# One decode step of attention and a gated feed-forward layer on one core: output weights in eight pieces, feed-forward weights behind all values, down projection in rows

## Chip, cores, metric

The kernel runs on one core of one Trainium2 chip. The metric is device time in microseconds (us) of one execution; most quoted times are medians of 4 to 9 runs. A ratio is the mean time of one kernel's runs over that of the other's runs of the same rounds, so it is not quite the ratio of the medians quoted. Each comes with a 95% interval, and the intervals here are about ±0.13% (±1.7 us) wide.

## The reference

Batch 4, one query token, 32 heads of width 128, 8192 cached keys and values per head, all in bf16. The formulas are shortened from the reference.

```python
def _A_ref(x, k_cache, v_cache, wq, wo):            # D = 512, H = 32, Dh = 128, Sk = 8192
    q = (x @ wq).reshape(B, 1, H, Dh).transpose(0, 2, 1, 3)
    scores = jnp.einsum("bhqd,bhkd->bhqk", q, k_cache) * (Dh ** -0.5)
    o = jnp.einsum("bhqk,bhkd->bhqd", _softmax(scores), v_cache)
    return o.transpose(0, 2, 1, 3).reshape(B, 1, H * Dh) @ wo

def _B_ref(x, w_gate, w_up, w_down):                # F = 1792
    return (_sigmoid(x @ w_gate) * (x @ w_up)) @ w_down

h  = x + _A_ref(_layernorm(x), k_cache, v_cache, wq, wo)
h2 = h + _B_ref(_layernorm(h), w_gate, w_up, w_down)
```

The caches are 537 MB and everything else is 14 MB: 128 key tiles and 128 value tiles of 2 MB each (one per batch and head), 4 MB each of query and output weights, 1.8 MB each of gate, up and down weights.

## The kernel before

All big loads are issued by one queue (the sync engine, SP), in the order of the list `items`. Keys, values and most weights go through a ring of eight 2 MB slots; the load of an item waits until the earlier tenants of its slot have been used up. A value is loaded ten steps (`LAG`) behind the key of the same head. The output weights are put where the transposed keys were (`kT`), so their load waits for the last score.

```python
        items = [("wq", 0)]
        for t in range(NT + LAG):                   # NT = 128, LAG = 10
            if t < NT:
                items.append(("k", t))
            if t == NT + 3:
                items.append(("wo", 0))             # after value 120
            if t == NT + LAG - 1:
                items.append(("wg", 0))             # ahead of the last value
            if t >= LAG:
                items.append(("v", t - LAG))
        items += [("wu", 0), ("wd", 0)]
        # ... ring slots ...
            if kind == "wo":
                return [(lambda e: e.dma_start(wo_v, A_wo.rearrange("(h p) f -> p h f", p=128)).then_inc(s_wo, 16),
                         s_wo, 16)]
            # ... the last value (127) comes in four pieces, all else in one load each ...
        for it in items:
            for op in dma_of[it]:
                op.deps = [sc_of[NT - 1]] if it[0] == "wo" else [consumed[p] for p in prev_of[it]]
```

The end of the program works on transposed activations: a feature on a partition, the batch of 4 in the columns. So in the down projection the weights are the stationary operand and only 4 columns move; the sum is added to `h`, turned round by four transposes, and cast.

```python
        def pe_down(e):
            mm = None
            for c in range(NDC):                    # 4
                for t in range(NFT):                # 14
                    mm = e.matmul(bX[:, B * c:B * c + B], wd_v[:, t, 128 * c:128 * (c + 1)],
                                  hh_sb[:, B * t:B * t + B], start=(t == 0), stop=(t == NFT - 1))
            return mm
        p_d = P("pe", pe_down, [d_hh, dma_of[("wd", 0)][0], d_st])
        d_o = P("dve", lambda e: e.tensor_tensor(oT_f[:, :], h2[:, 0, :], bX[:, 0:NB], ALU.add), [p_d])
        # ... pe_oT: four transposes of oT_f into bP[0] ...
        d_out = P("dve", lambda e: e.tensor_copy(o_sb[:, :], bP[0][0:B, 0:D]), [p_oT])
```

Of the kernel before, what the change touches and what calls it, by code (L numbers as in the profile page):

```python
# [6 lines left out]
FP32 = mybir.dt.float32  # L7
U32 = mybir.dt.uint32
ALU = mybir.AluOpType
ACT = mybir.ActivationFunctionType  # L10
AX = mybir.AxisListType

GH = 8
LAG = 10
# [58 lines left out]
def bass_sequential_preLN__mha_block_cached__glu_gated_glu__decode_kernel(  # L73
# [12 lines left out]
    B, _sq, D = A_x.shape  # L86
    _, H, S, DH = A_k_cache.shape
# [3 lines left out]
    NDC = D // 128  # L91
    NFT = F // 128
    NT = B * H
    NG = NT // GH
    R = S // 128
    TW = R * 128
# [4 lines left out]
    P = prog.add  # L101

    with ExitStack() as es:
        def SB(name, shape, dt):
            return es.enter_context(nc.sbuf_tensor(name, shape, dt))
# [9 lines left out]
        identf = SB("identf", [128, 128], FP32)  # L115
# [6 lines left out]
        x_bf = SB("x_bf", [128, D], BF16)  # L122
# [13 lines left out]
        h2 = SB("h2", [128, 2, NDC * B], FP32)  # L136
# [2 lines left out]
        hnT = SB("hnT", [128, NDC * B], BF16)  # L139
        sg_sb = SB("sg_sb", [128, NFT * B], FP32)  # L140
        hh_sb = SB("hh_sb", [128, NFT * B], BF16)
        oT_f = SB("oT_f", [128, NDC * B], FP32)
        o_sb = SB("o_sb", [B, D], BF16)

        PS = es.enter_context(nc.psum_tensor("PS", [128, 4096], FP32))
# [1 line left out]
        bS, bO, bP = bank[0:2], bank[2:4], bank[4:6]  # L147
        bX, bH = bank[6], bank[7]

        sems = {e: SEM("s_" + e) for e in _Prog.ENGS}  # L150
        s_x = SEM("s_x")
        s_out = SEM("s_out")
        s_wo = SEM("s_wo")
        s_slot = [SEM(f"s_slot{i}") for i in range(NS)]
        s_piece = [SEM(f"s_piece{i}") for i in range(4)]

        def ringv(slot):
            return ring[:, slot, :]


        items = [("wq", 0)]
        for t in range(NT + LAG):
            if t < NT:
                items.append(("k", t))
            if t == NT + 3:
                items.append(("wo", 0))
            if t == NT + LAG - 1:
                items.append(("wg", 0))
            if t >= LAG:
                items.append(("v", t - LAG))  # L170
        items += [("wu", 0), ("wd", 0)]
        slot_of, prev_of, dma_of = {}, {}, {}
        owner = [None] * (NS - 1) + [("qr", 0)]
        uses = [0] * NS
# [12 lines left out]
        consumed = {}  # L187
# [3 lines left out]
        wo_v = kT[:, :, :].rearrange("p s f -> p (s f)").rearrange("p (h f) -> p h f", h=H)  # L191
        wg_v = ringv(slot_of[("wg", 0)])[:, 0:NDC * F].rearrange("p (c f) -> p c f", c=NDC)
        wu_v = ringv(slot_of[("wu", 0)])[:, 0:NDC * F].rearrange("p (c f) -> p c f", c=NDC)
        wd_v = ringv(slot_of[("wd", 0)])[:, 0:NFT * D].rearrange("p (t f) -> p t f", t=NFT)

        def kv_src(t, cache):
            return cache[t // H, t % H, :, :].rearrange("(p r) d -> p (r d)", p=128)

        dma_x = P("sp", lambda e: e.dma_start(x_bf[0:B, :], A_x.rearrange("b s d -> (b s) d")).then_inc(s_x, 16),
                  sem=s_x, val=16)  # L200

        def load(it):
            kind, t = it
            slot = slot_of.get(it)
            if kind == "wo":
                return [(lambda e: e.dma_start(wo_v, A_wo.rearrange("(h p) f -> p h f", p=128)).then_inc(s_wo, 16),
                         s_wo, 16)]
            if kind == "v" and t == NT - 1:
                ops = []
                for i in range(4):  # L210
                    def f(e, i=i):
                        c0 = i * (TW // 4)
                        return e.dma_start(ringv(slot)[:, c0:c0 + TW // 4],  # L213
                                           kv_src(t, A_v_cache)[:, c0:c0 + TW // 4]).then_inc(s_piece[i], 16)
                    ops.append((f, s_piece[i], 16))
                return ops
            uses[slot] += 1
            sem, val = s_slot[slot], 16 * uses[slot]
            if kind == "k":
                dst, src = ringv(slot), kv_src(t, A_k_cache)  # L220
            elif kind == "v":
                dst, src = ringv(slot), kv_src(t, A_v_cache)
            elif kind == "wq":
                dst, src = wq_v, A_wq.rearrange("(c p) f -> p c f", p=128)
            elif kind == "wg":
                dst, src = wg_v, B_w_gate.rearrange("(c p) f -> p c f", p=128)
            elif kind == "wu":
                dst, src = wu_v, B_w_up.rearrange("(c p) f -> p c f", p=128)
            else:
                dst, src = wd_v, B_w_down.rearrange("(t p) f -> p t f", p=128)  # L230
            return [(lambda e: e.dma_start(dst, src).then_inc(sem, 16), sem, val)]  # L231


# [72 lines left out]
        for half in range(2):  # L306
            for a in range(4):
                def f(e, half=half, a=a):
                    dst = bass.AP(ring, QR0 + half * 2048 + 32 * a,
                                  [[NS * TW, 128], [256, 8], [128, 2], [1, 32]])  # L310
                    src = bS[half][:, :].rearrange("p (g w e) -> p g e w", g=8, e=2)
                    if half == 0:
                        return e.activation(dst, src, ACT.Copy)
                    return e.tensor_copy(dst, src)  # L314
# [15 lines left out]
        for b in range(B):  # L330
            ops = []
# [54 lines left out]
        def pe_pv(t, r0=0, r1=R, last=True):  # L386
            it = ("v", t)
            g, hh = t // GH, t % GH
            slot = slot_of[it]
            ob = bO[(g + (1 if t == NT - 1 else 0)) % 2]  # L390

            def f(e):
                mm = None
                for r in range(r0, r1):
                    c0 = (r % 16) * 32 + (r // 16) * 8 + hh
                    mm = e.matmul(ob[:, hh:hh + 1], ringv(slot)[:, r * 128:(r + 1) * 128],  # L396
                                  PT_sb[:, g % 2, c0:c0 + 1], start=(r == 0), stop=(r == R - 1))
                return mm
            deps = [ptc_of[g]]
            if t == NT - 1:  # L400
                deps += [dma_of[it][r0 // 16]]
            else:
                deps += dma_of[it]
            if hh == 0:
                deps.append(oev_of.get(g - 2))
            if t == NT - 1:
                deps.append(oev_of.get(g - 1))
            op = P("pe", f, deps)
            if last:
                pv_of[t] = op  # L410
                consumed[it] = op
# [105 lines left out]
        def wo_mms(e, heads, b0, b1, first=False):  # L517
            mm = None
            for h in heads:
                for c in range(NDC):  # L520
                    mm = e.matmul(bH[:, c * B + b0:c * B + b1], wo_v[:, h, 128 * c:128 * (c + 1)],
                                  OT[:, b0 * H + h:(b1 - 1) * H + h + 1:H],
                                  start=(first and h == heads[0] and c == 0),
                                  stop=(h == H - 1 and c == NDC - 1), skip_group_check=True)
            return mm
        gl = NG - 1
        P("pe", lambda e: wo_mms(e, range(0, H - GH), 0, B, True), [oev_of[gl - 1], dma_of[("wo", 0)][0], d_xnT])
        if B > 1:
            P("pe", lambda e: wo_mms(e, range(H - GH, H), 0, B - 1), [oev_of[gl - 1]])
        o_a = oev(gl, 0, GH - 1)  # L530
        P("pe", lambda e: wo_mms(e, range(H - GH, H - 1), B - 1, B), [o_a])
        P("act", lambda e: e.activation(lnst[0:B, 9:10], lnst[0:B, 3:4], ACT.Sqrt), [exp_of[gl]])
        for i in range(4):
            pe_pv(NT - 1, 16 * i, 16 * i + 16, last=(i == 3))
        o_b = oev(gl, GH - 1, GH)
        p_attn = P("pe", lambda e: wo_mms(e, range(H - 1, H), B - 1, B), [o_b])

# [21 lines left out]
                                                  mean_b(20), ALU.mult), [d_rs, d_hc])  # L559
        P("act", lambda e: e.activation(lnst[0:B, 10:11], tst[0:B, 12:13], ACT.Sigmoid), [a_sq])  # L560

        def pe_gu(e, wv, bk):
            mm = None
            for t in range(NFT):
                for c in range(NDC):
                    mm = e.matmul(bk[:, B * t:B * t + B], wv[:, c, 128 * t:128 * (t + 1)],
                                  hnT[:, B * c:B * c + B], start=(c == 0), stop=(c == NDC - 1))
            return mm
# [2 lines left out]
        a_sig = P("act", lambda e: e.activation(sg_sb[:, :], bS[0][:, 0:NFT * B], ACT.Sigmoid), [p_g])  # L571
        d_hh = P("dve", lambda e: e.tensor_tensor(hh_sb[:, :], sg_sb[:, :], bS[1][:, 0:NFT * B], ALU.mult), [a_sig, p_u])

        def pe_down(e):
            mm = None
            for c in range(NDC):
                for t in range(NFT):
                    mm = e.matmul(bX[:, B * c:B * c + B], wd_v[:, t, 128 * c:128 * (c + 1)],  # L578
                                  hh_sb[:, B * t:B * t + B], start=(t == 0), stop=(t == NFT - 1))
            return mm  # L580
        p_d = P("pe", pe_down, [d_hh, dma_of[("wd", 0)][0], d_st])
        d_o = P("dve", lambda e: e.tensor_tensor(oT_f[:, :], h2[:, 0, :], bX[:, 0:NB], ALU.add), [p_d])

        def pe_oT(e):
            mm = None
            for c in range(NDC):
                mm = e.transpose(bP[0][0:B, 128 * c:128 * (c + 1)], oT_f[:, B * c:B * c + B], identf[:, :])  # L587
            return mm
        p_oT = P("pe", pe_oT, [d_o, ptc_of[gl], ptc_of[gl - 1]])
        d_out = P("dve", lambda e: e.tensor_copy(o_sb[:, :], bP[0][0:B, 0:D]), [p_oT])  # L590
        consumed[("wg", 0)] = consumed[("wu", 0)] = consumed[("wd", 0)] = p_d

        def sp_out(e):
            e.dma_start(out.rearrange("b s d -> (b s) d"), o_sb[:, :]).then_inc(s_out, 16)
            return e.wait_ge(s_out, 16)
        P("sp", sp_out, [d_out])

        for it in items:
            for op in dma_of[it]:
# [51 lines left out]
```

## Time and profile before

The first lines are from the page of the kernel before: the span of the profiled execution, the busy time of the engines, the row of the queue that fetches instructions (packets, MB, share of the time of the 16 DMA engines), and the chain of work that ended last, by engine.

```profile
span 1314.9 us, 24889 instructions
PE 522.6 (40%) x11846; PEld 327.6 (25%) x11846; DVE 629.1 (48%) x640; ACT 38.9 (3%) x86; POOL 9.7 (1%) x17
...
q8 instruction: 92, 1.51, 0.5%
...
DMA 82%; DVE 12%; issue 3%; SPq 2%; PE 1%
```

The chain is 82% DMA, and TensorE and VectorE are busy less than half of the time. A kernel that is bound like this, and has to load the same bytes, gets faster in two ways only: the DMA engines must lose less time, or less must be left to do after the last byte.

The next two lines are the DMA view of 1180 to 1316 us in 40 slices of 3.4 us: busy tenths of the DMA engines, and GB/s.

```profile
DMA  9999999999999995699975999999999999998300
GB/s 429 419 424 429 436 429 414 429 429 419 439 424 424 429 424 246 252 393 381 366 251 192 354 437 429 434 419 429 429 429 411 398 396 390 411 388 292 138 0 1
```

There are two holes, at slices 16 and 17 (about 1231 to 1238 us) and at slices 21 and 22 (1248 to 1255 us). The timeline of the same kernel shows the issues that belong to them (start, duration, engine, load):

```profile
1235.66 0.38 SPq L206 DMA_DIRECT2D kT<-in_A_wo_dram  x1
1236.08 20.89 SPq L231 DMA_DIRECT2D ring<-in_A_v_cache_dram  x6
```

The output weights are issued only when the last score is done (1235.66 us), and all loads behind them in the queue wait too. Of the six value loads in the second line, the first alone holds the queue for 18.3 us, until 1254.4 us. By then 3298 of the 4096 rows (1 KB each) of the output weights have started in the trace; that its descriptors wait for theirs to drain is my reading.

The holes invite the thought that some 6 us of loading are lost there (four slices of 3.4 us at a mean of 235 instead of 428 GB/s). The trace holds one more thing that says otherwise. Each load leaves sixteen completion records, one per DMA engine. (The Trainium skill, "DMA: Bandwidth & Descriptors", section "Why a DMA increments its semaphore by 16 and not by 1", says that each of the sixteen engines adds one when its share has landed.) Sorted, they read as follows in the kernel before:

| load | first eight engines land (us) | last eight engines land (us) |
|---|---|---|
| key 0 | 18.0 to 18.1 | 18.2 to 18.6 |
| value 119 | 1226.3 to 1232.4 | 1241.8 to 1244.0 |
| value 120 | 1231.2 to 1237.2 | 1246.7 to 1249.0 |
| output weights | 1249.8 to 1250.1 | 1257.8 to 1260.0 |
| value 121 | 1261.0 to 1261.8 | 1262.8 to 1264.9 |
| value 127, last piece | 1295.1 to 1296.2 | 1298.6 to 1300.2 |
| up weights | 1299.6 to 1300.7 | 1303.3 to 1304.8 |
| down weights | 1304.7 to 1305.7 | 1308.0 to 1309.4 |

Eight engines run ahead of the other eight (the records do not name the engine; that it is the same eight each time is inferred from the order). From the first to the last it is 17.7 us at value 119. Both holes are idle time of the early half. The late half goes from load to load without a gap: while the holes last (1231.5 to 1236.6 and 1249.5 to 1254.4 us) the packets keep the 16 engines 59 and 54% busy, about nine of them. A load counts only when its last engine has landed. I call the two groups the early and the late half.

Last, the chain of waits from 1285 us on (start, duration, what):

```profile
1285.71 23.72 DMA ring<-in_B_w_down_dram
1309.44 0.14 issue
1309.57 1.65 PE PS L578 x56
...
1311.24 0.18 DVE oT_f L582
...
1311.47 1.02 PE PS L587 x4
...
1312.52 0.68 DVE o_sb L590
```

After the down weights have landed (1309.44 us) there are 1.65 us of down projection (56 matmuls), 0.18 of addition, 1.02 of transposes and 0.68 of cast. The output is issued at 1313.23 us, 3.79 us after the landing.

### The profile page before, as it was taken

Reading aid. Unit: us, or ns where it says so; the run is one execution under the profiler, and the core shown is the slowest. Engines: PE = TensorE matmul, PEld = TensorE weight load, DVE = VectorE, ACT = ScalarE, POOL = GpSimd, SP = SyncE. Lnnn points to the kernel's source line nnn. Section 1 sums busy time; section 2 is a strip of 40 time slices with the busy share of each in tenths; the row PEclk is TensorE's granted clock in tenths of the full one; section 3 lists DMA queues with packets and bytes.
Section 4 is the critical chain, followed back from the end, with each engine's and each line's share of the span. In section 5 each row is a group of like instructions: output and inputs, shape, how many; then the busy total and the mean of one; then the engine's idle time right before and its main releaser. Section 6 shows DMA issues by size and latency. Waiting matters only on the chain.

```text
span 1314.9 us, 24889 instructions
## 1 busy us (share of the span) xinstructions
PE 522.6 (40%) x11846; PEld 327.6 (25%) x11846; DVE 629.1 (48%) x640; ACT 38.9 (3%) x86; POOL 9.7 (1%) x17
## 2 busy tenths in 40 slices
PE   2453443433343353343344344344334434334425
PEld 1122222222232232222222222222222223222324
DVE  6975445445444544544544454554544444454300
ACT  3000000000000000000000000000000000000000
POOL 2000000000000000000000000000000000000000
DMA  9999999999999999999999999999999999999997
GB/s 391 428 427 426 428 426 428 426 426 427 427 427 427 428 427 425 427 427 428 426 427 428 427 426 428 426 428 427 426 427 427 426 428 425 429 426 428 371 381 292
DMA packets 44917, 552.37 MB, mean 420 GB/s; under 512 B 4232, under 2 KB 10128, under 8 KB 11664
## 3 DMA queue, kind: packets, MB, share of 16 engines
q1 hardware_dynamic: 44816, 550.79, 99.1%
q8 instruction: 92, 1.51, 0.5%
q14 instruction: 9, 0.07, 0.0%
HBM read 550.77 MB, written 0.00 MB: 419 GB/s over the span
## 4 chain that ended last, share of the span: by engine, by line
DMA 82%; DVE 12%; issue 3%; SPq 2%; PE 1%
DMA ring<-in_A_k_cache_dram 77%; DVE kT L356 11%; DMA ring<-in_A_v_cache_dram 2%; DMA ring<-in_B_w_down_dram 2%; SPq L213 1%; DMA ring<-in_A_wq_dram 1%; DVE Lq L339 0%; SPq L231 0%; PE PS L396 0%; PE PS L373 0%; PE PS L297 0%; DVE ring L314 0%; PE PS L324 0%; PE PS L578 0%; PE PS L587 0%
## 5 line engine op out<-in xcount | busy, mean ns | idle before, releaser
L356 DVE STREAM_TRANSPOSE kT<-ring 128x1024 uint32<-128x1024 uint32 x512 | 592.3, 1213 | 596.0 <-DMA ring<-in_A_k_cache_dram 596.0
L373 PE MATMUL PS<-kT,Lq 128*32 128x512 bf16 x2048 | 242.8, 623 | 663.5 <-DVE kT L356 663.5
L396 PEld LDWEIGHTS PS<-PT_sb,ring 128*128 128x128 bf16 x8192 | 230.1, 104 | 116.1 <-issue 75.5
L396 PE MATMUL PS<-PT_sb,ring 128*128 128x1 bf16 x8192 | 239.3, 165 | 39.7 <-DMA ring<-in_A_v_cache_dram 36.5
L373 PEld LDWEIGHTS PS<-kT,Lq 128*32 128x32 bf16 x2048 | 56.8, 126 | 751.3 <-DVE kT L356 679.8
L435 ACT ACTIVATE negm<-PS 128x1 f32<-128x1 f32 x16 | 2.7, 171 | 1166.9 <-PE PS L431 1166.9
L446 PE MATMUL PS<-LS,onesf 128*128 128x8 f32 x32 | 9.5, 372 | 65.2 <-DVE LS L442 65.2
L468 DVE TENSOR_TENSOR OT<-PS,rinv 128x8 bf16<-128x8 f32 (+2 forms) x17 | 2.0, 115 | 53.4 <-PE PS L396 53.4
L446 PEld LDWEIGHTS PS<-LS,onesf 128*128 128x128 f32 x32 | 8.0, 311 | 66.8 <-DVE LS L442 66.8
L457 PE MATMUL PS<-Sel,E_sb 128*32 128x32 bf16 x1024 | 11.4, 193 | 2.5 <-issue 1.4
L414 DVE TENSOR_REDUCE mx<-PS 128x1 f32<-128x512 f32 x16 | 10.5, 657 | 2.0 <-PE PS L373 2.0
L431 PEld LDWEIGHTS PS<-onesf,rowx 1*128 1x128 f32 x32 | 8.0, 307 | 12.6 <-issue 12.6
L437 ACT ACTIVATE E_sb<-PS,negm 128x512 bf16<-128x512 f32 x16 | 11.0, 687 | 0.7 <-ACT negm L435 0.2
L463 ACT ACTIVATE PT_sb<-PS 128x512 bf16<-128x512 f32 x16 | 9.6, 597 | 27.0 <-PE PS L457 27.0
L457 PEld LDWEIGHTS PS<-Sel,E_sb 128*32 128x32 bf16 x1024 | 9.6, 103 | 2.8 <-issue 1.5
L431 PE MATMUL PS<-onesf,rowx 1*128 1x1 f32 x32 | 9.3, 358 | 0.0
L249 POOL MEMSET Lq<- 128x8208 f32 x1 | 6.9, 6937 | 0.0
L339 DVE CAST Lq<-PS 32x128 bf16<-32x128 f32 x8 | 5.7, 712 | 2.2 <-PE PS L324 2.0
L267 DVE TENSOR_SCALAR xpad<-x_bf,lnst 4x512 bf16<-4x512 bf16 x1 | 6.0, 5993 | 0.0
L420 PE MATMUL PS<-identf,mx 128*1 128x128 f32 x16 | 5.9, 371 | 0.0
L314 DVE CAST ring<-PS 128x512 bf16<-128x512 f32 x4 | 2.5, 684 | 7.2 <-PE PS L297 7.2
L338 ACT ACTIVATE Lq<-PS 32x128 bf16<-32x128 f32 x8 | 5.7, 715 | 4.3 <-PE PS L324 4.1
(69 smaller groups left out, 67.5 us busy)
## 6 DMA issues: line engine op xcount, KB each, us to landing
ring<-in_A_k_cache_dram SPq DMA_DIRECT2D x128, 2048.0 KB, 34.7
ring<-in_A_v_cache_dram SPq DMA_DIRECT2D x127, 2048.0 KB, 35.9
ring<-in_A_wq_dram SPq DMA_DIRECT2D x1, 4096.0 KB, 12.5
kT<-in_A_wo_dram SPq DMA_DIRECT2D x1, 4096.0 KB, 24.3
ring<-in_A_v_cache_dram SPq DMA_DIRECT2D x4, 512.0 KB, 28.0
ring<-in_B_w_gate_dram SPq DMA_DIRECT2D x1, 1792.0 KB, 37.8
ring<-in_B_w_up_dram SPq DMA_DIRECT2D x1, 1792.0 KB, 23.4
ring<-in_B_w_down_dram SPq DMA_DIRECT2D x1, 1792.0 KB, 23.7
```

Of the source, the lines that this page charges most:

```text
L213: return e.dma_start(ringv(slot)[:, c0:c0 + TW // 4], kv_src(t, A_v_cache)[:, c0:c0 + TW // 4]).then_inc(s_piece[i], 16)
L249: zlq = pool(lambda e: e.memset(Lq[:, :].bitcast(FP32), 0.0))
L267: d_x = P("dve", lambda e: e.tensor_scalar(xpad[0:B, :], x_bf[0:B, :], st[0:B, 0:1], st[0:B, 4:5], op0=ALU.subtract, op1=ALU.mult), [d_r, zx])
L356: return e.transpose(kT[:, buf, i * q:(i + 1) * q].bitcast(U32), ringv(src)[:, i * q:(i + 1) * q].bitcast(U32))
L373: mm = e.matmul(bS[g % 2][32 * j:32 * (j + 1), :], Lq[:, l0:l0 + 32], rhs, start=(hh == 0 and v == 0), stop=(hh == GH - 1 and v == 3), til ...
L396: mm = e.matmul(ob[:, hh:hh + 1], ringv(slot)[:, r * 128:(r + 1) * 128], PT_sb[:, g % 2, c0:c0 + 1], start=(r == 0), stop=(r == R - 1))
L414: mx_of[g] = P("dve", lambda e: e.tensor_reduce(mx[:, :], bS[g % 2][:, :], AX.X, ALU.max), [sc_of[g * GH + GH - 1], p1_of.get(g - 1)])
L431: p2_of[g] = P("pe", lambda e: e.matmul(bX[:, 0:1], rowx[0:1, :], onesf[0:1, 0:1], start=True, stop=True), [d2b_of[g], c_ones])
L437: exp_of[g] = P("act", lambda e: e.activation(E_sb[:, :], bS[g % 2][:, :], ACT.Exp, bias=negm[:, 0:1], scale=SCALE, accum_out=sig[:, 0:1]) ...
L446: L_of[g] = P("pe", lambda e: e.matmul(bX[:, 0:GH], onesf[:, :], LS[:, :], start=True, stop=True), [LS_of[g], a1_of[g], c_ones])
L457: mm = e.matmul(bP[g % 2][32 * a:32 * (a + 1), 32 * rr:32 * rr + 32], E_sb[:, 32 * rr:32 * rr + 32], Sel[:, a, :], start=True, stop=True, ...
L463: ptc_of[g] = P("act", lambda e: e.activation(PT_sb[:, g % 2, :], bP[g % 2][:, :], ACT.Copy), [pt_of[g]] + last_pv)
```

## The change

Its intent: fill the holes (output weights in eight pieces between the last values, so that no value is stuck behind 4096 descriptors), let the last value come before the feed-forward weights, and shorten the end (no transposes: the down projection makes rows of the output directly, on top of `h`, which TensorE has put into the same accumulator beforehand; ten of the fourteen tiles of the down weights can be used before the rest has landed). The core of the diff, with cuts:

```diff
+        WD_PARTS = [(0, 10), (10, NFT)]
+        NWO = 8
+        HW = H // NWO
         ...
             if t < NT:
                 items.append(("k", t))
-            if t == NT + 3:
-                items.append(("wo", 0))
-            if t == NT + LAG - 1:
-                items.append(("wg", 0))
             if t >= LAG:
                 items.append(("v", t - LAG))
-        items += [("wu", 0), ("wd", 0)]
+            if NT + 1 <= t <= NT + NWO:
+                items.append(("wo", t - NT - 1))
+        items += [("wg", 0), ("wu", 0), ("wd", 0)]
         ...
-        dma_x = P("sp", lambda e: e.dma_start(x_bf[0:B, :], ...
+        dma_x = P("act", lambda e: e.dma_start(x_bf[0:B, :], ...
         ...   (wo: eight loads of four heads; value 127: two pieces instead of four; wd: two loads)
+        def pe_h(e):
+            mm = None
+            for s_ in range(2):
+                for c in range(2):
+                    k = 2 * s_ + c
+                    mm = e.matmul(bP[s_][0:B, 128 * c:128 * (c + 1)], h2[:, 0, B * k:B * k + B], identf[:, :],
+                                  start=(c == 0), stop=False, skip_group_check=True)
+            return mm
         ...
-        (pe_down in 56 matmuls, d_o, pe_oT, d_out)
+        p_d = []
+        for i, (t0, t1) in enumerate(WD_PARTS):
+            for s_ in range(2):
+                def pe_down(e, t0=t0, t1=t1, s_=s_):
+                    mm = None
+                    for t in range(t0, t1):
+                        mm = e.matmul(bP[s_][0:B, 0:HD], hh_sb[:, B * t:B * t + B], wd_v[:, t, HD * s_:HD * s_ + HD],
+                                      start=False, stop=(t == NFT - 1), skip_group_check=True)
+                    return mm
+                p_d.append(P("pe", pe_down, [d_hh, dma_of[("wd", 0)][i]]))
+        o0 = P("act", lambda e: e.activation(o_sb[:, 0:HD], bP[0][0:B, 0:HD], ACT.Copy), [p_d[2]])
+        o1 = P("dve", lambda e: e.tensor_copy(o_sb[:, HD:D], bP[1][0:B, 0:HD]), [p_d[3]])
```

In the new form the four columns of `hh` are the stationary operand and 256 columns (HD) of the weights move, in 28 matmuls.

## The prediction

> **What bounds the kernel now.** The page of the profile shows 552 MB at a mean of 420 GB/s, DMA share 9 in all slices but the last; the chain of waits is 82% DMA. So only lost DMA time and the work after the last byte can be won. The sixteen completion records of each load split the DMA engines into two halves: early they land together (18.0 to 18.6 us), but value 120 lands on eight engines at 1231-1237 us, on the other eight at 1247-1249. I put the drift down to instruction fetches (92 packets of 16 KB) on one half. The late half has no gap: value 120 at 1249.0, output weights 1260.0, value 121 at 1264.9, ..., last piece of the last value 1300.2, up weights 1304.8, down weights 1309.4. It sets the end.
>
> **The loads.** In the DMA table by slices the rate falls to 190-250 GB/s at about 1230-1237 and 1247-1254 us: the large output-weight load waits for the last score (1235.7), and the next value's issue is stuck 18.3 us behind its descriptors. Eight pieces cure the second hole, but both are idle time of the early half, off the critical path. The first even grows by one value (4.9 us), since the first piece queues behind value 119 instead of 120; the late half still has work until about 1244. Reordering leaves the late half's sum unchanged. Small terms: query weights issue 0.4 us earlier (-0.4); 1 KB descriptors run at 46 instead of 43.5 ns beside a busy other half (estimate, +0.4); six more completions (+0.3). Last byte: 1309.7 instead of 1309.4.
>
> **The tail after it.** Before (timeline): landing 1309.44, 56 matmuls with 4 moving columns to 1311.22 (28 ns each), add 0.17, transposes 1.0, cast 0.68, output issue 1313.23: 3.8 us. The change removes add, transposes and half of the cast, but makes the down projection 28 matmuls that stream 256 columns. The score matmuls stream 512 and start, in groups of four side by side, every 0.427 us in all 128 bursts, so 256 cost about 0.213 us (estimate). The Trainium skill ("TensorE: Matmul & The Clock Gate", Part 1) gives 1.2 GHz for a cold array and 2.4 after some 3.4 us of sustained work; the trace agrees with the cold figure (512 columns in 0.427 us) and shows no faster burst. 28 x 0.213 = 6.0 us against 1.6. The first 20 can start about 1.4 us before the last landing: -1.4 + 0.1 + 6.0 + 0.2 drain + 0.5 cast = 5.4 us until the output's issue when cold, about 2.4 if warm throughout. I take 4.8, as the array may warm within the burst: +1.0. Adding h in PSUM and the later feed-forward weights sit in slack.
>
> **Sum.** +1.0 (tail) +0.3 (last byte) = +1.3: 1318.3 us, range 1315.4 to 1320.4. Chances: faster by over 2% 0.01, within 2% 0.98, slower 0.01.
>
> **What would show it.** Right: the second rate hole is gone, the first longer; the last landing within 1 us of 1309.4; down-projection matmuls spaced 0.21 us or falling to 0.11; output issue 4 to 5.4 us after the landing. Wrong: the last landing moves by several us (the hole had slowed the late half), or matmuls at 0.11 us from the start (about 1316).
>
> **What would make it wrong.** A warm array (-2.5); the late half running dry behind the pieces' waits (several us); an instruction fetch stalling the tail (+2).

## The result and the profile after

The changed kernel took 1317.93 us (median of 4 runs, 1317.60 to 1318.59) against 1317.01 us (median of 4, 1316.99 to 1317.26); ratio 1.0007, interval 0.999 to 1.0024. By the interval that is "the same". All four runs of the change are slower than all four of before, so the sign is probable.

The lines of the page that answer to those above:

```profile
span 1316.8 us, 24848 instructions
PE 527.4 (40%) x11822; PEld 330.1 (25%) x11822; DVE 628.7 (48%) x639; ACT 39.2 (3%) x87; POOL 9.7 (1%) x17
...
q8 instruction: 92, 1.51, 0.5%
...
DMA 85%; DVE 12%; issue 2%; PE 1%; SPq 0%
```

The profiled run was the slowest of the four (1318.59 us), so its span is 1.9 us longer, while the medians differ by 0.9. The DMA slices of 1180 to 1316 us:

```profile
DMA  9999999999999754699999999999999999988400
GB/s 439 419 424 426 429 419 429 434 424 429 429 419 429 337 241 212 246 425 397 425 398 423 404 418 401 409 405 397 427 383 422 389 414 406 387 300 270 143 4 1
```

The second hole is gone and the first has become longer (slices 14 to 17 instead of 16 and 17), as the first piece of the output weights now queues behind value 119 and not behind value 120. The issues:

```profile
1235.67 0.38 SPq L207 DMA_DIRECT2D kT<-in_A_wo_dram  x1
1236.09 0.51 SPq L241 DMA_DIRECT2D ring<-in_A_v_cache_dram  x1
...
1237.11 3.69 SPq L241 DMA_DIRECT2D ring<-in_A_v_cache_dram  x1
```

No value load holds the queue for 18 us any more; the longest of these takes 6.0. Still, the landings of the late half at the end are where they were: up weights at 1305.3 us (before: 1304.8), last part of the down weights at 1310.05 (before: 1309.44). The chain from there:

```profile
1286.08 22.63 DMA ring<-in_B_w_down_dram
1308.70 0.14 issue
1308.84 5.76 PE PS L602 x28
...
1314.62 0.41 DVE o_sb L607
```

The first part of the down weights lands at 1308.70 us, 28 matmuls take 5.76 us, and the output is issued at 1315.13, 5.08 us after the last landing (before: 3.79). What the transposes gave, the long stream took.

The windows view of the down-projection line alone shows how (stretch in us, its length, busy time of TensorE and number of matmuls, the same for weight loads, granted clock, DMA share, GB/s):

```profile
1309.50:1310.50 1.00, 1.00 (x6) 0.57 (x5) 0.50 0.00 1
1310.50:1311.50 1.00, 1.00 (x6) 0.64 (x5) 0.50 0.00 0
1311.50:1312.50 1.00, 1.00 (x7) 0.59 (x5) 0.50 0.00 0
1312.50:1313.50 1.00, 1.00 (x7) 0.57 (x6) 0.50 0.00 0
1313.50:1314.60 1.10, 1.08 (x7) 0.54 (x5) 0.75 0.00 0
```

Six to seven matmuls per us (0.213 us each) while the clock record says 0.50; it turns to full at 1314.05 us, when only the last three matmuls are still to start, and those are 0.11 us apart.

### The profile page after: what moved, and what is told of

It is laid out like the page before. It is cut to its first block, busy times and chain, and to the rows that moved or that the text cites. A ratio compares the mean times of both kernels' runs of the same rounds, so it can differ in the third digit from the quotient of the medians.

```text
span 1316.8 us, 24848 instructions
## 1 busy us (share of the span) xinstructions
PE 527.4 (40%) x11822; PEld 330.1 (25%) x11822; DVE 628.7 (48%) x639; ACT 39.2 (3%) x87; POOL 9.7 (1%) x17
## 4 chain that ended last, share of the span: by engine, by line
DMA 85%; DVE 12%; issue 2%; PE 1%; SPq 0%
DMA ring<-in_A_k_cache_dram 77%; DVE kT L366 11%; DMA ring<-in_A_v_cache_dram 6%; DMA ring<-in_B_w_down_dram 2%; DMA ring<-in_A_wq_dram 1%; PE PS L602 0%; DVE Lq L349 0%; PE PS L406 0%; PE PS L307 0%; DVE ring L324 0%; PE PS L383 0%; PE PS L334 0%; SPq L241 0%; SPq L207 0%; DVE o_sb L607 0%
## 5 line engine op out<-in xcount | busy, mean ns | idle before, releaser
L467 PE MATMUL PS<-Sel,E_sb 128*32 128x32 bf16 x1024 | 11.4, 192 | 2.8 <-issue 1.7
L602 PE MATMUL PS<-ring,hh_sb 128*4 128x256 bf16 x28 | 5.7, 397 | 1.8 <-DMA ring<-in_B_w_down_dram 1.8
```

Source lines behind the costliest of these rows:

```text
L467: mm = e.matmul(bP[g % 2][32 * a:32 * (a + 1), 32 * rr:32 * rr + 32], E_sb[:, 32 * rr:32 * rr + 32], Sel[:, a, :], start=True, stop=True, ...
```

## The experiments

My theory has three parts. (1) The loads' new order is nearly neutral, because it only rearranges the idle time of the early half. (2) The loss is the stream of 256 columns per matmul on a TensorE at half clock. (3) The halves drift apart because of instruction fetches. The rivals: the pieces of 1 KB rows slow the stream and the tail is neutral; or the holes were worth their bytes and something else took the gain; or eight engines are simply slow.

The table sums up the profiled run of each kernel; "tail" is the time from the last landing of the down weights to the issue of the output. The runs before that shared a chip with these had medians of 1316.88 to 1317.01 us.

| run | last landing (us) | tail (us) | median time (us), runs | ratio to before, interval |
|---|---|---|---|---|
| before | 1309.44 | 3.79 | 1317.01 (4) | |
| the change | 1310.05 | 5.08 | 1317.93 (4) | 1.0007, 0.999 to 1.0024 |
| after_again | 1310.01 | 3.62 | 1317.90 (5) | 1.0008, 0.9995 to 1.002 |
| loads_only | 1310.21 | 3.79 | 1317.11 (5) | 1.0, 0.9987 to 1.0014 |
| tail_only | 1309.67 | 4.58 | 1318.20 (5) | 1.001, 0.9997 to 1.0022 |
| rows_tiled | 1310.00 | 1.39 | 1314.83 (5) | 0.9984, 0.9972 to 0.9997 |
| half_pv | 1304.22 | 4.82 | 1312.59 (4) | 0.9965, 0.9951 to 0.9979 |
| wo_1_sooner | 1309.93 | 4.65 | 1317.94 (4) | 1.0008, 0.9992 to 1.0023 |
| wo_2_sooner | 1313.95 | 4.16 | 1321.59 (4) | 1.0036, 1.0022 to 1.005 |
| cols_parts | 1309.74 | 2.66 | 1315.86 (5) | 0.9992, 0.9979 to 1.0004 |
| down_on_8 | 1320.3 | 2.1 | 1324.97 (5) | 1.0061, 1.0048 to 1.0075 |
| x_on_sp | 1310.26 | 4.86 | 1318.12 (5) | 1.001, 0.9997 to 1.0022 |
| before_tiled | 1309.72 | 1.39 | 1314.58 (5) | 0.9983, 0.997 to 0.9995 |
| rows_tiled_2 | 1309.46 | 1.40 | 1314.77 (5) | 0.9983, 0.997 to 0.9997 |

All twelve passed the comparison with the reference.

### after_again: the change once more

No edit.

> The changed kernel once more, beside the others of this call. Expected: 0.6 to 1.3 us slower than before (1317.6 to 1318.4), last landing of the down weights within 0.7 us of 1309.7, first landing group to output issue as before. In its trace: 28 down-projection matmuls spaced 0.213 us until the clock record turns to full, then 0.11. If the array gets warm early in this run, the time is nearer to 1316.

Measured: 1317.90 us, 1317.09 to 1318.52. The nine runs of the change so far scatter over 1.5 us, the nine of before over 0.5 us. The windows of this second trace show why (the same view as above):

```profile
1309.50:1310.50 1.00, 1.00 (x7) 0.58 (x6) 0.50 0.00 0
1310.50:1311.50 1.00, 1.00 (x7) 0.66 (x6) 0.64 0.00 0
1311.50:1312.50 1.00, 1.00 (x12) 0.78 (x10) 1.00 0.00 0
1312.50:1313.50 1.00, 0.58 (x6) 0.24 (x3) 1.00 0.00 0
```

Here the clock turned at 1311.2 us, 2.6 us after the stream began, and twelve matmuls passed in the next us. The output was issued 3.62 us after the last landing; in the other trace 5.08. The landings of the two traces differ by 0.04 us, so the whole difference of 1.5 us between the two spans (1316.8 and 1315.3) is where the clock's turn fell. This profiled run was the fastest of its five (1317.09 us), the profiled run of the first result the slowest of its four (1318.59): the turn of the clock is worth about as much as the whole scatter. My figure of 1316 for an early turn was too low, as the first half of the stream still ran at half clock.

### loads_only and tail_only: the change in two parts

`loads_only` is the change with the old down projection, transposes and cast and one load of the down weights; `tail_only` is the kernel before with the new down projection and the two parts of the down weights.

```diff
 loads_only, against the change
-        (pe_h; pe_down in rows; o0, o1; wd in two loads)
+        (pe_down in 56 matmuls; d_o; pe_oT; d_out; wd in one load)
 tail_only, against before
-        (pe_down in 56 matmuls; d_o; pe_oT; d_out; wd in one load)
+        (pe_h; pe_down in rows; o0, o1; wd in two loads)
```

> The new order and pieces of the loads, with the old down projection, transposes and one load of the down weights. My theory (the loads are nearly neutral because the late half of the DMA engines sets the end; the loss is in the tail): 0 to +0.6 us against before, last landing 1309.4 to 1310.0, output issue 3.8 us after it. Rival (1 KB descriptors between the values slow the stream, the tail is neutral): the whole +0.9 us is here, with the last landing 1 us or more later. Second rival (the hole in the rate was worth its bytes): 2 to 3 us faster than before.

> The loads as before (one load of output weights, gate weights before the last value, x on the sync queue), but the down weights in two parts and the down projection in rows on top of h. My theory: last landing 1309.4 to 1309.8, output issue 5.0 to 5.4 us after it, so +1.2 to +1.8 us against before (1318.2 to 1318.8). Rival (the loads cost, the tail is neutral): within 0.3 us of before.

Measured: `loads_only` 1317.11 us, +0.2 against its before (1316.88), tail 3.79 as before; `tail_only` 1318.20 us, +1.3. So the loss sits in the tail, and the eight pieces, the hole they fill and the hole they lengthen make no difference that these runs resolve. The first rival (pieces cost, tail neutral) and the second (the holes were worth 2 to 3 us) both fall. The tail of `tail_only` was 4.58 us, shorter than the 5.0 to 5.4 I expected; in its trace the clock turned 4.2 us into the stream.

### rows_tiled: the same rows, side by side

The down projection keeps its form, but the output is cut into four quarters of 128 columns, each on its own 32 columns of the array (the Trainium skill, "TensorE: Matmul & The Clock Gate", Part 3, describes this packing; score matmuls use it already, and in the trace the matmuls of each group of four start within 14 ns).

```diff
-                    for t in range(t0, t1):
-                        mm = e.matmul(bP[s_][0:B, 0:HD], hh_sb[:, B * t:B * t + B], wd_v[:, t, HD * s_:HD * s_ + HD], ...)
+                for t in range(t0, t1):
+                    for j in range(NDC):
+                        mm = e.matmul(bP[0][32 * j:32 * j + B, 0:128], hh_sb[:, B * t:B * t + B],
+                                      wd_v[:, t, 128 * j:128 * (j + 1)], start=False, stop=(t == NFT - 1),
+                                      tile_position=(0, 32 * j), skip_group_check=True)
+        (pe_h with the same tile positions; four casts of 128 columns, two on ScalarE, two on VectorE)
```

> The change, but the down projection in four column tiles side by side (each 128 output columns on its own 32 columns of the array), so one group of four streams 128 columns in about 0.107 us cold: 14 groups take 1.5 us instead of 6.0, and four casts of 128 columns follow, two on each of two engines. My theory: output issue 1.2 to 1.6 us after the last landing, so 3.5 to 4 us faster than the change and 2 to 3 us faster than before (1314 to 1315). If the cost of the rows is not their streaming (but the wait for the first part, the casts, the two banks), it stays within 1 us of the change.

Measured: 1314.83 us, 3.1 us under the change and 2.1 under before, interval clear of 1. Its timeline:

```profile
1308.61 1.24 PE L599 MATMUL PS<-ring,hh_sb 128*4 128x128 bf16 x40 [1.84 <-DMA ring<-in_B_w_down_dram]
1310.05 0.59 PE L599 MATMUL PS<-ring,hh_sb 128*4 128x128 bf16 x16 [0.20 <-DMA ring<-in_B_w_down_dram]
1310.69 0.56 ACT L608 ACTIVATE o_sb<-PS 4x128 bf16<-4x128 f32 x2 [6.97 <-PE PS L599]
1310.69 0.60 DVE L608 CAST o_sb<-PS 4x128 bf16<-4x128 f32 x2 [3.60 <-PE PS L599]
1311.39 0.35 SPq L613 DMA_DIRECT2D out_dram<-o_sb  x1
```

Forty matmuls take 1.24 us and are done before the second part lands (1310.00); the last sixteen take 0.59, the casts 0.60, and the output goes out 1.39 us after the landing. The two parts of the down weights and `h` in the accumulator are as in the change; the columns that stream one after another were cut from 28 x 256 to 14 x 128. One accumulator bank instead of two and four casts of 128 columns instead of two of 256 came along, but the casts took longer than in the change (0.60 against 0.41 us) and the matmuls alone went from 5.76 us to 1.24 and 0.59. That is the intervention that shows the streaming half of part (2); the share of the clock shows in the two traces of the change itself (0.213 and 0.11 us a matmul, tails of 5.08 and 3.62 us). The run scatter was 0.2 us here (1314.69 to 1314.90), but 0.7 us when the same kernel ran again (`rows_tiled_2`), so a smaller scatter is not shown.

### cols_parts: the old form with the down weights in two parts

```diff
 against the change: the old pe_down, d_o, pe_oT and d_out, but
+            for i, (t0, t1) in enumerate(WD_PARTS):      # 40 matmuls, then 16
+                ... start=(t == 0 and c == 0) ... [d_hh, dma_of[("wd", 0)][i], d_st]
```

> The change's loads, down weights in two parts, but the old form of the down projection (56 matmuls of 4 columns, 28 ns each), 40 of them before the last part lands; then add, transposes and cast as before. My theory: output issue 0.1 + 0.45 + 0.2 + 0.2 + 1.05 + 0.7 = 2.6 to 2.8 us after the last landing, so 1.0 to 1.2 us faster than loads_only (about 1316.0). If the split of the down weights gained nothing, it would equal loads_only (1317.1).

Measured: 1315.86 us and a tail of 2.66 us, 1.25 us under `loads_only`. So loading the down weights in two parts is worth about 1.2 us by itself, and it was in the change; the new form of the matmuls ate this and more.

### half_pv: fewer instructions, the same loads

Wrong result on purpose: every second matmul of the value product is left out. (It still passed the comparison, which is no proof that it is right; probably the attention output is small beside `x`.)

```diff
-                for r in range(r0, r1):
+                for r in range(r0, r1, 2):
```

> Wrong result on purpose: the changed kernel with every second matmul of the value product left out, all loads kept. TensorE is not the bound, so only the instruction stream changes: some 8200 of 24848 instructions fewer. My theory (the drift of eight DMA engines is instruction fetches): instruction packets fall from 92 to about 62, the spread between early and late half at value 119 falls from about 16 us by a third to 10 to 11 us, the last landing moves from 1310.0 to 1305 to 1306, and the time falls by 4 to 5 us to about 1313.5. Rival (eight engines are simply slower): same spread, same last landing, same time.

The lines of its page that matter (span and instructions; the queue that fetches instructions):

```profile
span 1310.7 us, 16656 instructions
...
q8 instruction: 60, 0.98, 0.3%
```

Measured: 60 instruction packets instead of 92, spread at value 119 from 1226.4 (first engine) to 1237.8 (last) instead of 1226.0 to 1243.7, so 11.4 us instead of 17.7: the spread fell to 64%, the packets to 65%. The early half landed when it always does; the late half came 5.9 us sooner. The last landing moved by 5.8 us and the time by 5.3. This is what part (3) says, and the rival (eight engines are simply slower) had the same spread. (The Trainium skill, "Runtime: NRT & Kernel Launch", section "Instruction fetch mechanics", says that instructions come in blocks of 16 KiB over a DMA queue of the sequencer's own and that this cost is mostly hidden. The block size agrees: all 92 packets have 16384 bytes. The cost to the loads is not hidden in this kernel.) The records do not name the DMA engine of a packet, so that nearly all fetches fall on the late eight is inferred, not seen.

One rival remains: with half of the value matmuls, TensorE also reads less from the on-chip memory that the loads write to. The completions and the fetch packets of the traces speak against it. Take for each load the sum over the sixteen engines of the lag behind the first engine, and see how it grows from one key or value to the next (of those issued before 1200 us; a fetch is counted when it starts before the load's ninth landing and after that of the load before):

| trace | steps without a fetch: number, mean growth (us) | steps with one fetch: number, mean growth (us) |
|---|---|---|
| before | 161, 0.09 | 84, 1.50 |
| the change | 161, 0.08 | 84, 1.53 |
| half_pv | 192, 0.05 | 54, 1.53 |

So the lag comes with the fetches, one by one, and each costs the same 1.5 us with all value matmuls or with half of them. Over nine tenths of the lag is in the late eight (129.4 of 140.0 us in before).

### wo_1_sooner and wo_2_sooner: a longer hole, in two steps

```diff
-            if NT + 1 <= t <= NT + NWO:
+            if NT <= t < NT + NWO:              # wo_1_sooner; wo_2_sooner: NT - 1 <= t < NT - 1 + NWO
```

> The change with the output-weight pieces queued one value sooner (first piece behind value 118 instead of 119). All loads behind it wait for the last score at 1235.7. My theory: the early half idles 4.9 us longer, but the late half still has value 118 until about 1238.8 while the first piece starts at about 1237.5, so the last landing stays within 0.5 us of 1310.0 and the time within 0.5 us of the change (1317.9). Rival (idle time of the early half costs its bytes): half of 4.9, i.e. 2.4 us slower.

> The same, two values sooner (first piece behind value 117). My theory: the late half is done with value 117 at about 1234 and idles until the first piece starts at about 1237.5, so now the time is lost: last landing 3 to 4 us later than 1310.0, time about 1321 to 1322. Rival (idle time of the early half costs its bytes): 4.9 us slower than the change, evenly from step to step (1322.8).

The rates of the two, the same 40 slices of 1180 to 1316 us, first one sooner, then two sooner:

```profile
GB/s 434 414 434 422 434 429 419 429 424 434 429 419 246 241 207 212 233 437 388 431 393 436 388 436 391 419 394 411 410 407 417 410 417 401 405 397 360 210 2 1
```

```profile
GB/s 419 439 410 441 429 414 429 429 424 429 361 222 236 202 217 43 108 436 407 437 378 442 388 417 401 423 395 399 420 402 427 414 439 395 410 403 407 374 301 38
```

One value sooner, the early half idles for five slices (207 to 246 GB/s) and nothing is lost: last landing 1309.93 us, time 1317.94 against 1317.93 and 1317.90. Two values sooner, the late half runs dry too (slices at 43 and 108 GB/s), the last landing comes 3.9 us later and the time is 1321.59, 3.7 us slower. A cost of the idle early half would have come evenly, 2.4 us a step; there was none at the first step. This shows part (1): a hole at half rate is free here as long as the late half keeps work, and a hole in which that half idles too is not.

### x_on_sp: the small input load back on the sync queue

```diff
-        dma_x = P("act", ...
+        dma_x = P("sp", ...
```

> The change with the small input load back on the sync queue, ahead of the query weights. My theory: query weights issue 0.4 us later and every landing of the late half moves by 0.4 us; last landing 1310.4, time about 1318.3, 0.4 us slower than the change, less than the change's own scatter of 1.5 us. If the start of the stream were not on the critical path: no shift of the landings at all.

Measured: last landing of the late half 1310.26 us (the change: 1310.05 and 1310.01), at value 119 1244.0 (1243.7), time 1318.12, 0.2 us slower than the change. The shift is half of the 0.4 us that I expected, and neither it nor its absence is shown: six traces with this order of the loads scatter over 0.75 us in their last landing, and the change's times over 1.5 us.

### down_on_8: half of the down weights on eight engines

If the late half is the bottleneck, some of its bytes could go to the early half. By the rule in the Trainium skill ("DMA: Bandwidth & Descriptors", section "Why a DMA increments its semaphore by 16 and not by 1", "How many engines (k)") a load with 8 partitions runs on the lowest-numbered eight engines. (The trace agrees on the eight: each of the sixteen small loads left eight landings and one record at its issue, 144 in all. Which eight, it does not name.) In `rows_tiled`, seven of the fourteen tiles of the down weights were loaded that way, from ScalarE's queue:

```diff
+        for m in range(16):
+            ... e.dma_start(wd_v[8 * m:8 * m + 8, NFT // 2:NFT, :], B_w_down...[8 * m:8 * m + 8, NFT // 2:NFT, :])
+            dma_wd8.append(P("act", f, [pv_of[NT - 6]], s_piece[3], 16 * 16))
```

> The tiled version with the last seven tiles of the down weights loaded by 16 small loads of 8 partitions each, issued from ScalarE's queue once value 122 is used; the Trainium skill (DMA: Bandwidth & Descriptors, how many engines) says that such a load runs on the lowest-numbered 8 engines only. If those 8 are the early half: the late half is relieved of 56 descriptors of 1 KB, last landing about 1307.5 to 1308.3 instead of 1310.0, output issue 1.5 to 1.8 us after it, time about 1313 (1.5 to 2 us under rows_tiled's 1314.83). If they are the late half, it gets 112 instead of 56 of these: last landing about 1312.5, time about 1317.5. If both halves share them, within 0.5 us of rows_tiled.

Measured: 1324.97 us, 10 us slower than `rows_tiled`, outside all three expectations. The last load of the down weights on the sync queue (the other seven tiles) landed on two engines at 1308.7 to 1309.2, on twelve at 1312.7 to 1313.8 and on two at 1319.4 to 1320.3. That looks as if the eight loaded engines were six of the early half and two of the late; then, if the rule holds, the early half is not the lowest eight. Each small load of 1 KB rows also cost more than the estimate from their 46 ns, and the sync queue's loads behind it came late on all sixteen engines. Why the size is so large was not settled.

### before_tiled and rows_tiled_2: the short tail on the old loads

`before_tiled` is `tail_only` with the tiled down projection; `rows_tiled_2` is `rows_tiled` again on the same chip.

```diff
 before_tiled, against before
-        (pe_down in 56 matmuls; d_o; pe_oT; d_out; wd in one load)
+        (pe_h and pe_down in four column tiles; four casts; wd in two loads)
```

> The kernel before with all its loads where they were (one output-weight load, gate weights before the last value), only the down weights in two parts and the down projection in four column tiles on top of h. My theory: the new order of the loads is worth nothing or costs a few tenths, so last landing about 1309.6, output issue 1.4 us later, time 1314.3 to 1314.9, level with or up to 0.5 us under rows_tiled_2. If the new order of the loads is of use once the tail is short, it is over 0.5 us slower than rows_tiled_2.

> rows_tiled again, for the comparison on one chip: 1314.6 to 1315.0, scatter under 0.3 us as there is no long stream of matmuls that meets the clock's turn at a different place each time.

Measured: 1314.58 and 1314.77 us. The scatter of `rows_tiled_2` was 0.7 us (1314.31 to 1315.00), not under 0.3 as I had expected. The two are level within these runs, both clear of before (intervals 0.997 to 0.9995 and 0.997 to 0.9997). The new order of the loads is worth nothing with the short tail either. Both are versions that beat the kernel before and the change.

## Why the prediction was right, point by point

The predicted time was 1318.3 us (1315.4 to 1320.4), the measured one 1317.93, and 1317.90 the second time. The range is five times as wide as the effect (0.9 us), so that the time lies in it says little; what counts is whether the steps hold.

- **The late half sets the end, so the reordering does not count.** Right: `loads_only` +0.2 us, `wo_1_sooner` no loss, `wo_2_sooner` a loss as soon as the late half ran dry, `before_tiled` level with `rows_tiled_2`.
- **The drift comes from instruction fetches.** It was only a guess when written ("I put the drift down to"); `half_pv` bears it out in proportion and the table of fetches step by step. The size comes out too, but not from the 1.07 us that a fetch packet took in the profile (92 of them on eight engines would be 12.3 us each): a fetch cost an engine 1.5 us, and the late eight were 129.4 / 8 = 16.2 us further behind the first engine at value 117 than at key 0 (the last of them 17.6 us behind). Why 1.5 and not 1.07 stays open.
- **Last byte at 1309.7.** Measured 1310.05 in the profiled run. Over six traces with the new loads the mean is 1309.9, over three with the old ones 1309.6, so the sum of the small terms (+0.3) fits, though the six scatter over 0.75 us. Of its terms, the 1 KB rows and the completions of the pieces (+0.4 and +0.3) can be seen only together: from each piece's landing less that of the load before it, the late eight spent 11.4 to 11.9 us on average (mean of the traces 11.7) on the eight pieces in these six traces, against 11.3 on the single load in the three others, so +0.4. The third (-0.4, query weights issued earlier) is not shown (`x_on_sp`). That the three add up to the measured sum may be luck.
- **28 matmuls at 0.213 us on a cold array, falling to 0.11 if it warms.** Right on both, in seven of seven traces with this tail.
- **Tail of 4.8 us.** The seven traces with this tail have 3.62 to 5.08, mean 4.5. The uncertain part was when the clock turns, and it turned 2.6 to 5.2 us after the stream's start. So the prediction's +1.0 for the tail was of the right size (4.5 - 3.8 = 0.7), and its spread was a fair one.
- **What would show it wrong.** The condition "output issue 4 to 5.4 us after the landing" failed in one trace (3.62), for the reason that the prediction had named, an earlier warm array.

What the change expected and did not get: the filled hole was off the critical path; about 1.2 us from the two parts of the down weights and 1.2 us of addition and transposes (0.18 + 1.02) were real, but streaming 256 columns 28 times at half clock cost more than both.

## What to carry to other kernels

When a kernel is bound by DMA, look at the sixteen completions of each load, and not only at the rate: a hole that only the early engines see costs nothing, and filling it gains nothing. After the last byte count the columns that TensorE must stream one after another, at the clock it will have there (half here, after a wait), and put small outputs side by side on the array rather than in one long row. A stream of a few us after a wait can also bring scatter: in two traces of the same kernel the clock turned 2.6 and 5.2 us into it, and the tails were 1.5 us apart.

## What the Trainium skill lacked or had wrong

- "Runtime: NRT & Kernel Launch", "Instruction fetch mechanics", calls the cost of crossing a 16 KiB block "mostly hidden". That is said of the instructions; the page lacks what a fetch costs the loads of a kernel that saturates the DMA engines: each delayed one engine by about 1.5 us, and 32 packets fewer (60 instead of 92) made the kernel 5.3 us faster (1312.59 against the change's 1317.9), since they seem to fall almost only on half of the DMA engines. That page and "DMA: Bandwidth & Descriptors" lack that the engines drift apart by 17.7 us in 1240 us of such a stream.
- "TensorE: Matmul & The Clock Gate", Part 1, says that what is issued in the first 3.4 us runs at half clock and everything after at full clock. Its two rates agree (0.213 and 0.11 us for 256 columns), and its windows of 3413 ns are in the clock records. But the turn came 2.6, 3.3, 4.2, 4.3, 4.6, 4.8 and 5.2 us after the start of the stream in seven traces, so up to 5.2 us ran cold (the 3.3 is from the spacing of the matmuls of `wo_2_sooner`, 0.213 and then 0.11 us from 1316.1 us on, as its trace has no clock records). The same paragraph calls the window free-running, and so read the six recorded turns fit: the stream filled 77 to 100% of the 3.41 us before each turn, and at most 53% of the 3.41 us before those. A budget of 3.4 us from the first matmul on is then too simple.
- The same page lacks that matmuls with few moving columns do not keep the clock up, though the profile shows TensorE as busy: after the query projection of the change the record shows full clock from 16.99 to 20.40 us and then half, while TensorE streamed 4-column matmuls 26 ns apart from 17.4 to 19.0 and 19.5 to 21.2 us. In `after_again` they filled 85% of such a window (17.58 to 20.99 us) and the clock fell, while 256-column matmuls that filled 77% of one brought it up.
- "DMA: Bandwidth & Descriptors" (same section, "How many engines (k)") gives a rule for the engines of an 8-partition load but not what such loads cost beside a saturated queue: sixteen of them (112 rows of 1 KB per engine) made the kernel 10 us slower (1324.97 against 1314.83); the cause of that size is open.
